# Halved first loads and transposes, tile 1's scores in two sets, and a new order for the opening of a fused attention and MLP kernel

## The chip, the cores and the metric

The kernel runs on one core of a Trainium2 chip. The metric is device time in microseconds (us) of one execution. Before the change three runs took 198.22, 198.23 and 198.53 us, median 198.23.

## The reference

The computation has two parts in a row: an attention in which each query sees 96 local keys and 8 global ones, with a bias that falls with distance, and an MLP with a squared ReLU. Its sizes are 4 batches, 8 heads, 768 positions, head size 64; the MLP has 3072 tokens, 512 columns and 2048 hidden columns.

```python
scores = scale * np.matmul(q, k.transpose(0, 1, 3, 2))
is_global = pos[None, :] < int(n_global)
is_local = (rel >= 0) & (rel < int(n_local))
keep = is_global | is_local
dist = np.where(is_global & ~is_local, float(n_local), np.abs(rel))
bias = -slopes[:, None, None] * dist[None, :, :]
scores = np.where(keep, scores + bias, -1000000000.0)
a = softmax(scores)
x = np.matmul(a, v)            # heads side by side: 3072 x 512
h = x @ w_in
g = np.maximum(h, 0.0) ** 2
return g @ w_out
```

## The kernel before

The 3072 positions are 24 tiles of 128 rows (six per batch). Tile j has its own keys and those of tile j-1, and the eight global keys of its batch; the first tile of a batch (0, 6, 12, 18) has its own keys alone. Two tiles make a block of 256 tokens for the MLP, so there are 12 blocks.

For a tile, the steps are: load q, k and v (fp32 in memory, bf16 on the chip); transpose q and k so that the head size is on the partitions (`tr` on TensorE, here PE, line 530, and the copies `T` out of PSUM, line 546 through the helper of line 416); scores (`sc`, line 619); exp on ScalarE, ACT (`exp`, line 685); for tiles from 3 on a product with a table E of biases on VectorE, DVE (`mul`, line 710); a matmul with v (`pv`, line 769); the division by the sum (`norm`, lines 799 and 800); the transpose of the result x for the MLP (`trx`, line 837, and the copy `xT`). The first three tiles have no product with E: their bias is added on PE (`bias`, line 599) by matmuls of scaled identities `sid` (lines 377 to 382) with a table of distances, in the same PSUM banks as the scores. Each tile takes over eight global keys and values by small copies (`gk`, `gv`).

The MLP of blocks 0 and 1 is computed step by step: a step (`s1`) takes 256 hidden columns of a block, 8 matmuls of 256 columns each or 16 of 128 (line 1083), then `relu` and `sq` evacuate it (lines 886 and 1120); a step needs its piece of w_in, which is loaded in 8 pieces of 256 KB (two of them in two halves). The later blocks use sums of weight parts (`isum`, `wsum`) and seven products in place of eight (`h`, `u`, `c`, `q`, then `s2`).

Tile 0 and 1 differ from the rest: their q and k come over the SP queue as fp32 (lines 319 to 321), 512 KB each, into memory that later holds weight sums (wsum), are cast to bf16 by `cast` (two halves of columns for each of q and k), and are transposed two tiles at a time: 16 transposes for q and 16 for k, then four copies. All other loads are issued by GpSimd (POOL), which casts on the way, and also computes some of the `gv` copies in the same queue.

The order of everything is written out in the table ORDER (lines 57 to 160). Each word is an operation, with the engine behind @ (A for ACT, V for DVE, P for POOL) and the PSUM banks behind the colon; `T.1.3` is the copy of k (1; q is 0) of tile 3. A word adds its instructions to the end of its engine's queue, and each engine works through its queue in order. A word's place against words of other engines has no effect of its own: an instruction waits for its data, for its bank and for what stands ahead in its own queue.

Of the kernel before, what the change touches and what calls it, by code (L numbers as in the profile page):

```python
# [62 lines left out]
ld.win.4.0 ld.win.7.0 pv.2.0:7 pv.2.1:2 gv.2@P ld.win.5.0 ld.win.0.0 ld.win.2.0 tr.1.4:6 norm.2.0 norm.2.1 exp.3.0.0
T.1.4@V s1.0.1:4 s1.0.1#2 sc.4.0:0257 trx.2:3 s1.0.3:1 mul.3.0 relu.0.1@A T.1.5@A pv.3.0:6 mul.3.1 xT.2@V pv.3.1:4
s1.0.3#2 norm.3.0 gk.4@V norm.3.1 exp.4.0.1 exp.4.1.0 exp.4.0.0 exp.4.1.1 mul.4.0 mul.4.1 relu.0.3@A s1.0.4:2
sc.5.0:6547 trx.3:1 s1.0.7:3 xT.3@V sq.0.1@V relu.0.4@A gv.3@A exp.5.1.0 sq.0.3@A exp.5.1.1 s1.1.3:0 relu.0.7@V sq.0.4@A
exp.5.0.0 exp.5.0.1 relu.1.3@V gate.9 sq.0.7@V sq.1.3@A ld.v.4 ld.win.2.1 ld.win.6.0 ld.v.5 ld.win.0.1 s1.1.5:5 s1.1.4:7
# [5 lines left out]
isum.1.0 u.2.0.1@V xs.2.0 s1.1.0:7 tr.1.7:6 s2.0.0.0:2 sc.6.0:45 E0.1 relu.1.2@A u.2.1.1@A exp.6.0.0 exp.6.1.0
relu.1.0@V xs.2.1 sq.1.0@V sq.1.2@A T.1.7@A sq.1.1@V s1.0.6:1 h.2.0.p6 tr.0.7:4 h.2.1.p2:5 relu.0.6@A sq.0.6@A
s2.0.0.1:7 s2.0.1.1 h.2.1.p6 h.2.0.p2:6 s2.0.1.0 s2.0.2.0 mul.6.0 c.2.1.c11 isum.3.1 sum.1.0 c.2.0.c11 sum.1.1 u.2.1.2@A
s2.0.3.0 T.0.7@A sc.7.0:1645 h.2.1.p7 s2.0.2.1 s2.0.4.0 exp.7.0.0 u.2.0.2@A exp.7.0.1 exp.7.1.1 h.2.1.p5:1 s2.0.5.0
pv.6.0:4 s2.0.6.0 s2.0.7.0 isum.2.1 wsum.0.0 wsum.1.0 u.2.1.3@V c.2.1.c22 h.2.1.p3 wsum.0.1 wsum.1.1 xs.2.2 norm.6.0
s2.0.3.1 s2.0.4.1 s2.0.5.1 h.2.0.p7 s2.1.p1.0:5 s2.1.p1.1 s2.0.6.1 s2.0.7.1 s2.1.p2.0:4 o.0.0@A q.2.0.c11@A q.2.1.c11@A
u.2.0.3@A s2.1.p2.1 h.2.0.p4 part.1.p1@A exp.7.1.0 s2.1.p6.0 pv.6.1:2 s2.1.p6.1 part.1.p6@A s2.2.p1.0:6 h.2.1.p4
c.2.0.c21@A s2.2.p1.1 q.2.1.c22@A c.2.1.c12 sum.1.3 wsum.2.0 wsum.2.1 o.0.1@V q.2.0.c21@A c.2.1.c21@A q.2.1.c21@A  # L80
h.2.0.p5:7 o.1.p2 sum.1.2 mul.7.0 gate.11 st.0.0 load.9 T.9 load.8 T.8 load.11 s2.1.p7.0 norm.6.1 gate.12 gate.10
gate.14 mul.7.1 wsum.3.1 isum.2.0 pv.7.1:3 trx.6:1 wsum.3.0 s2.1.p7.1 xT.6@A s2.1.p5.0 gk.7@V c.2.0.c22 part.1.p7@A
pv.7.0:0 q.2.1.c12@A load.10 s2.1.p5.1 norm.7.0 gate.13 q.2.0.c22@A h.2.0.p3 gate.15 s2.1.p4.0 c.2.0.c12 s2.1.p4.1
o.1.p5 q.2.0.c12@A sc.8.0:7012 norm.7.1 o.1.p4@A s2.1.p3.0 sum.2.0 load.12 part.2.p1@A s2.1.p3.1 exp.8.1.0 trx.7:3
sum.2.1 exp.8.0.0 h.3.0.p1:5 exp.8.1.1 xT.7@V h.3.1.p1:0 o.1.p3 exp.8.0.1 h.3.0.p2:7 gk.8@V xs.3.0 u.3.1.1@A sc.9.0:2314
mul.8.0 u.3.0.1@A s2.2.p6.0 xs.3.1 exp.9.0.1 mul.8.1 T.10 h.3.0.p6 exp.9.1.1 h.3.1.p2:1 gv.7@V c.3.0.c11 exp.9.0.0
h.3.1.p6 st.0.1 c.3.1.c11 pv.8.0:4 st.1.1 u.3.1.2@A s2.2.p6.1 norm.8.0 pv.8.1:7 q.3.1.c11@A s2.2.p2.0:2 sum.2.2 gv.8@P
u.3.0.2@A h.3.1.p7 norm.8.1 exp.9.1.0 h.3.0.p5:1 part.2.p6@A xs.3.2 h.3.0.p7 xT.8 u.3.1.3@A mul.9.1 s2.2.p2.1
q.3.0.c11@A mul.9.0 h.3.1.p5:4 u.3.0.3@A st.1.0 s2.2.p7.0 c.3.1.c22 T.12 s2.2.p7.1 c.3.0.c22 pv.9.0:7 q.3.1.c22@A
h.3.1.p3 o.2.p2 q.3.0.c22@A h.3.0.p4 T.11 c.3.1.c12 h.3.0.p3 c.3.0.c21@A norm.9.0 s2.3.p1.0:3 part.2.p7@A s2.3.p1.1  # L90
c.3.0.c12 q.3.1.c12@A pv.9.1:4 h.3.1.p4 q.3.0.c12@A norm.9.1 h.4.0.p1:5 load.15 c.3.1.c21@A gk.9@V sum.3.0 s2.2.p5.0
xT.9 part.3.p1@A q.3.0.c21@A sc.10.0:7140 sum.3.1 s2.2.p5.1 exp.10.1.0 sum.2.3 s2.2.p4.0 exp.10.0.0 gk.10@V o.2.p5
s2.2.p4.1 exp.10.0.1 mul.10.0 load.13 h.4.0.p2:1 u.4.0.1@A s2.3.p6.0 exp.10.1.1 c.4.0.c11 h.4.1.p1:7 gv.9@A s2.2.p3.0
mul.10.1 o.2.p4@A s2.2.p3.1 q.3.1.c21@A sum.3.2 s2.3.p2.0:4 u.4.1.1@A load.14 pv.10.0:0 xs.4.0 pv.10.1:1 gate.17 o.2.p3
s2.3.p6.1 xs.4.1 norm.10.0 s2.3.p2.1 part.3.p6@A h.4.0.p6 q.4.0.c11@A norm.10.1 h.4.1.p6 gv.10@A sum.3.3 xT.10 s2.3.p7.0
u.4.0.2@A xs.4.2 sc.11.0:6201 o.3.p2 u.4.1.2@A h.4.0.p7 exp.11.1.0 st.2.0 h.4.1.p7 T.13 exp.11.0.0 u.4.0.3@V s2.3.p7.1
exp.11.1.1 gate.16 mul.11.0 sc.12.0:26 exp.11.0.1 h.4.0.p4 h.4.1.p2:1 mul.11.1 c.4.0.c21@A s2.3.p5.0 c.4.1.c11
exp.12.1.0 pv.11.0:0 pv.11.1:5 part.3.p7@A norm.11.0 s2.3.p5.1 q.4.1.c11@A h.4.0.p5:1 u.4.1.3@A norm.11.1 h.4.1.p5:6
q.4.0.c21@A gate.20 c.4.0.c22 xT.11 s2.3.p4.0 exp.12.0.0 s2.3.p4.1 gate.18 c.4.1.c22 load.16 h.4.0.p3 o.3.p5 T.15
q.4.1.c22@A h.4.1.p4 mul.12.0 q.4.0.c22@A h.4.1.p3 c.4.0.c12 s2.4.p2.0:0 o.3.p4@A c.4.1.c21@A c.4.1.c12 h.5.0.p1:5  # L100
st.3.1 st.2.1 s2.3.p3.0 u.5.0.1@A q.4.1.c12@V T.14 s2.3.p3.1 q.4.0.c12@A h.5.0.p2:2 o.3.p3 q.4.1.c21@A sc.13.0:1376
c.5.0.c11 h.5.1.p1:4 exp.13.0.0 xs.5.0 s2.4.p2.1 sum.4.0 exp.13.1.0 pv.12.1:2 s2.4.p1.0:1 q.5.0.c11@A xs.5.1 mul.13.0
pv.12.0:3 s2.4.p1.1 u.5.1.1@A gk.13@V sum.4.1 h.5.0.p6 exp.13.0.1 h.5.1.p6 exp.13.1.1 norm.12.0 h.5.0.p5:7 u.5.1.2@A
norm.12.1 h.5.1.p2:6 part.4.p1@A h.5.1.p5:3 xs.5.2 u.5.0.2@A xT.12 mul.13.1 h.5.1.p7 c.5.1.c11 h.5.0.p7 pv.13.0:2 st.3.0
sum.4.2 u.5.0.3@A s2.4.p6.0 T.16 gate.19 s2.4.p6.1 o.4.p2 u.5.1.3@A c.5.0.c22 h.5.0.p4 q.5.1.c11@A pv.13.1:6 norm.13.0
part.4.p6@A s2.4.p5.0 c.5.0.c21@A gv.13@P sum.4.3 h.5.0.p3 q.5.0.c22@A load.17 h.5.1.p4 norm.13.1 q.5.0.c21@A s2.4.p7.0
c.5.0.c12 xT.13 s2.4.p7.1 kl.15@V s2.4.p5.1 c.5.1.c22 part.4.p7@A sc.14.0:2567 q.5.0.c12@A o.4.p5 s2.4.p4.0 kl.14@V
exp.14.0.1 load.18 h.5.1.p3 q.5.1.c22@V c.5.1.c21@A s2.4.p4.1 exp.14.1.1 c.5.1.c12 h.6.0.p1:6 exp.14.1.0 mul.14.1
s2.4.p3.0 exp.14.0.0 s2.4.p3.1 o.4.p4@A mul.14.0 sc.15.0:4735 q.5.1.c12@A xs.6.0 u.6.0.1@A h.6.0.p2:2 xs.6.1 s2.5.p1.0:1
exp.15.0.0 o.4.p3 s2.5.p1.1 exp.15.1.0 c.6.0.c11 st.4.0 h.6.0.p6 exp.15.1.1 T.17 sum.5.0 h.6.0.p5:4 u.6.0.2@A pv.14.0:0  # L110
sum.5.1 pv.14.1:7 exp.15.0.1 h.6.1.p1:2 norm.14.0 part.5.p1@A gv.14@P h.6.0.p7 u.6.1.1@A xs.6.2 load.19 s2.5.p6.0
gate.21 sum.5.2 u.6.0.3@A h.6.1.p6 norm.14.1 q.6.0.c11@A s2.5.p6.1 mul.15.0 q.5.1.c21@A xT.14 h.6.0.p4 part.5.p6@A
# [1345 lines left out]
```

## Time and profile before

| | |
|---|---|
| median of three runs | 198.23 us |
| the profiled execution | 198.52 us |
| its span, first to last instruction | 196.8 us |
| PE busy | 189.8 us (96%) |
| DVE busy | 176.5 us (90%) |
| ACT busy | 163.1 us (83%) |
| POOL busy | 75.2 us (38%) |
| q0, the queue that POOL feeds | 74016 packets, 13.11 MB |
| granted TensorE clock | 0.998 |

All times below are from the start of the span. PE is TensorE's matmul row and PEld its weight load, which overlaps it. A timeline line has the start, the length, the engine, the source line, the operation, the tiles (out<-in), the size and the count; in brackets stands how long the engine had been idle before it and what ended that. When a line holds several instructions its length runs from the first start to the last end. A line of the DMA issues has the number of transfers, their size at the destination (the fp32 source of a cast load is twice as large), and the us from issue to landing.

### The profile page before, as it was taken

The numbers are of one execution on the slowest core, as the hardware profiler recorded it, in microseconds if no ns is written. First come the engines' busy times: TensorE is split into PE (matmuls) and PEld (weight loads), VectorE is DVE, ScalarE is ACT, GpSimd is POOL, SyncE is SP. The second block draws the span as 40 slices with busy tenths as digits, with TensorE's granted clock in tenths as the row PEclk, the third lists the DMA queues.
The fourth block names the chain that finished last, engine by engine and source line by source line (L and its number), as shares of the span: only waits on it lengthen the run. The fifth ranks groups of instructions, "written<-read, shape, count | busy, mean of one in ns | idle before, by whom it ended". The sixth has DMA issues, their size and how long they took to land.

```text
span 196.8 us, 6859 instructions
## 1 busy us (share of the span) xinstructions
PE 189.8 (96%) x2816; PEld 167.8 (85%) x2816; DVE 176.5 (90%) x427; ACT 163.1 (83%) x340; POOL 75.2 (38%) x94
## 2 busy tenths in 40 slices
...
DMA  5999999999699999999999999794996611114023
GB/s 161 194 177 188 183 172 171 205 195 182 112 118 155 189 194 126 190 140 186 140 130 169 110 148 172 166 172 71 115 76 132 160 37 53 30 27 158 5 103 113
DMA packets 105615, 27.18 MB, mean 138 GB/s; under 512 B 95088, under 2 KB 102768, under 8 KB 105584
## 3 DMA queue, kind: packets, MB, share of 16 engines
q0 software_dynamic: 74016, 13.11, 87.2%
...
## 4 chain that ended last, share of the span: by engine, by line
PE 81%; DMA 9%; DVE 5%; ACT 2%; issue 1%; POOL 0%; SPq 0%; DVEq 0%
PE bank L1234 31%; PE bank L972 29%; PE bank L1083 6%; PE bank L619 5%; PE bank L769 4%; PE bank L1365 4%; DMA win<-in_moe_w_in_dram 3%; DMA xT<-x 3%; DMA wsum<-in_k_dram 3%; DVE hsum L1189 1%; ACT at L685 1%; DVE xs L944 1%; ACT qkT L418 1%; DVE hr L1017 1%; DVE x L800 1%
## 5 line engine op out<-in xcount | busy, mean ns | idle before, releaser
L1037 ACT ACTIVATE hs<-hr 128x512 bf16<-128x512 f32 x72 | 44.7, 639 | 5.1 <-DVE hr L1017 4.7
L685 ACT ACTIVATE esc<-bank 128x512 bf16<-128x512 f32 x78 | 43.3, 619 | 1.8 <-PE bank L619 1.4
L1234 PE MATMUL bank<-wsum,hsum 128*128 128x256 bf16 x264 | 36.4, 273 | 0.0
L1234 PEld LDWEIGHTS <-hsum 128*128 128x128 bf16 x360 | 31.9, 98 | 3.5
L1017 DVE CUSTOM_DVE_ANT_0 hr<-bank,early 128x512 f32<-128x512 f32 x45 | 30.4, 685 | 2.2 <-PE bank L972 1.5
L972 PEld LDWEIGHTS <-qk_first 128*128 128x128 bf16 x480 | 29.7, 98 | 1.9 <-DVE xs L944 0.5
L972 PEld LDWEIGHTS <-win 128*128 128x128 bf16 x480 | 29.8, 98 | 1.0
L418 ACT COPY early<-bank 128x512 f32<-128x512 f32 x40 | 23.5, 592 | 4.4 <-PE bank L972 4.3
L710 DVE TENSOR_TENSOR at<-esc,E 128x1024 bf16<-128x1024 bf16 x39 | 26.6, 695 | 0.4 <-ACT esc L685 0.3
L1234 PEld LDWEIGHTS <-hs 128*128 128x128 bf16 x264 | 24.1, 98 | 2.6
L310 POOL DMA_DIRECT2D v<-in_v_dram x18 | 16.1, 892 | 25.0 <-DVE v L468 10.2
L1234 PE MATMUL bank<-wout,hs 128*128 128x256 bf16 x176 | 24.7, 273 | 0.0
L420 POOL COPY v<-v 8x520 bf16<-8x520 bf16 x7 | 5.3, 762 | 49.1 <-PE bank L769 45.4
L972 PE MATMUL bank<-xT,win 128*128 128x128 bf16 x320 | 23.6, 219 | 0.0
L972 PE MATMUL bank<-xs,qk_first 128*128 128x128 bf16 x320 | 22.8, 219 | 0.2 <-DVE xs L944 0.2
L310 POOL DMA_DIRECT2D qk<-in_q_dram x18 | 16.1, 897 | 15.5 <-DMA qkT<-qk 15.1
L800 DVE TENSOR_TENSOR x<-bank,rs 128x256 bf16<-128x256 f32 x48 | 20.4, 424 | 1.8 <-DVE rs L799 0.2
L886 ACT ACTIVATE hr<-bank 128x512 f32<-128x512 f32 x30 | 17.8, 594 | 0.7 <-PE bank L972 0.4
L418 ACT COPY part<-bank 128x256 f32<-128x256 f32 x29 | 10.8, 374 | 8.4 <-PE bank L1234 8.4
L769 PE MATMUL bank<-v,at 128*128 128x65 bf16 x352 | 17.4, 193 | 0.1
L310 POOL DMA_DIRECT2D qk<-in_k_dram x18 | 16.3, 906 | 0.4 <-DMA wout<-in_moe_w_out_dram 0.3
L1083 PE MATMUL bank<-xT,win 128*128 128x256 bf16 (+1 forms) x160 | 16.2, 251 | 0.2
...
## 6 DMA issues: line engine op xcount, KB each, us to landing
out_dram<-o SPq DMA_DIRECT2D x22, 256.0 KB, 3.7
v<-in_v_dram POOLq DMA_DIRECT2D x24, 128.0 KB, 5.2
qk<-in_q_dram POOLq DMA_DIRECT2D x18, 128.0 KB, 5.2
qk<-in_k_dram POOLq DMA_DIRECT2D x18, 128.0 KB, 5.3
wout<-in_moe_w_out_dram POOLq DMA_DIRECT2D x8, 256.0 KB, 8.4
win<-in_moe_w_in_dram POOLq DMA_DIRECT2D x6, 256.0 KB, 6.9
wsum<-in_q_dram SPq DMA_DIRECT2D x1, 512.0 KB, 4.2
wsum<-in_k_dram SPq DMA_DIRECT2D x1, 512.0 KB, 5.5
```

What stands on the lines that cost most here:

```text
L310: nc.gpsimd.dma_start(out=dst, in_=src)
L418: nc.scalar.copy(dst, src)
L685: nc.scalar.activation(out=tiles[tag, j, g][:, odd], in_=tiles.pop(("sc", j, odd, g)).rearrange("p a c -> p (a c)"), func=Act.Exp, scale=s ...
L710: nc.vector.tensor_mul(at, tiles.pop(("esc", j, g)), bias)
L769: nc.tensor.matmul(out=po[:, hi, :], lhsT=tiles["at", j, g][:, odd, at * P : (at + 1) * P], rhs=v_sb[kj][:, h, :], start=(i == 0), stop=(i ...
L800: nc.vector.tensor_tensor(out=x[:, 4 * hf : 4 * hf + 4, :], in0=po[:, :, :D], in1=rs.to_broadcast([P, 4, D]), op=Alu.mult,)
L886: nc.scalar.activation(dst, src, Act.Relu)
L972: nc.tensor.matmul(out=tiles["h", blk, g, bank][:, n], lhsT=left_[:, s, k], rhs=right_[:, k], start=opens and n == 0 and k == 0, stop=k == ...
L1017: nc.vector._custom_dve(TENSOR_ADD_SAT, out=hr, in0=src, in1=tiles.pop(("u", blk, g, i)), s0=float("inf"), s1=0.0,)
L1037: nc.scalar.activation(hs, hr, Act.Square)
L1083: nc.tensor.matmul(out=hT[:, c, cols], lhsT=w_in_sb[s][:, kt, c * P : (c + 1) * P], rhs=tiles["xT", blk][:, kt, cols], start=(kt == 0), st ...
L1234: nc.tensor.matmul(out=tiles["acc", blk, bank][:, cols], lhsT=left_[:, s], rhs=right_[:, cols], start=first and s == 0, stop=s == NSTEP - ...
```

## The change

Five things change, all in the opening of the kernel.

- The q and k of tiles 0 and 1 are loaded in four transfers of four heads each instead of two of eight: q, k, q, k. The order of casts is unchanged in kind, but each cast now waits only for its own half.
- Their transposes are split the same way: 8 for four heads in place of 16, into a bank of their own, and each copy `T` of a half has 256 columns instead of 512. The names get a fourth part, the half: `T.1.0.1` is the copy of k of tile 0, second half.
- Tile 1's scores, one set before, become two: `sc.1.0` for heads 0 to 3 and `sc.1.1` for heads 4 to 7, each waiting only for its own half.
- Four of the eight scaled identities are made by ACT instead of DVE.
- ORDER is written anew up to its 300th word of about 1220; from there on it is the same word for word, except for two loads.

```diff
 ORDER = """
-ld.k.2 ld.v.0 ld.q.2 ld.v.1 ld.q.4 ld.v.2 ld.k.4 ld.win.1.0 cast.0.1@V cast.0.0@V cast.1.0@V bias.0.0:46 bias.1.0:0152
...
+cast.0.0@V cast.1.0@V bias.1.0:47 tr.0.0.0:3 tr.1.0.0:5 bias.1.1:01 T.0.0.0@A T.0.1.0@A cast.0.1@A bias.0.0:23 ones.6
...
-    SETS = {}
+    SETS = {1: [(0,), (1,)]}
...
-    for n, src in ((0, q), (1, k)):
-        nc.sync.dma_start(out=plain[n].rearrange("p (h c) -> p h c", h=H), in_=rows_of_two(src, 0))
-        land["qk"[n], 0] = 4.5 + 1.1 * n
+    for i in range(2):
+        for n, src in ((0, q), (1, k)):
+            h = slice(i * H // 2, (i + 1) * H // 2)
+            nc.sync.dma_start(out=plain[n].rearrange("p (h c) -> p h c", h=H)[:, h], in_=rows_of_two(src, 0)[:, h])
+            land["qk"[n], i] = 4.5 + 1.1 * i + 0.5 * n
...
-    for h in range(H):
+    for h in range(H // 2):
+        nc.scalar.mul(sid[h], ident32, float(slopes[h] / scale))
+    for h in range(H // 2, H):
...
-                for i in range(2) if j == 0 else ():
+                for hs in (range(2), range(2, 4)) if j == 0 else (range(4),):
+                    at = (hs.start // 2,) if j == 0 else ()
...
-                    for pair in range(NPAIR):
+                        for pair in hs:
...
-                            e, qkT[j + i][:, n].rearrange("p a (c r) -> p a c r", r=2),
-                            tiles["tr", n, j][:, :, i * D : (i + 1) * D],
+                                e, qkT[j + i][:, n, h].rearrange("p a (c r) -> p a c r", r=2),
+                                tiles["tr", n, j, *at][:, h, i * D : (i + 1) * D],
...
-        deps = list(parts)
+        every = list(parts)
...
+            deps = [d for d in every if d is None or len(d["name"]) < 4 or d["name"][3] in gs or first]
```

The first place is the start of ACT's queue, from its first activation on (E is the bias table, `at` the exps of tiles 0 to 2, qkT the transposed q and k, wsum the memory that holds q and k as fp32). Before:

```order
L358 ACTIVATE junk<-early 128x1
L386 ACTIVATE E<-pb 128x256 x8
L418 CAST qk_first<-wsum_96 128x512
L418 COPY qkT_81<-bank_110 128x512
L685 ACTIVATE at<-bank_111 128x512
L685 ACTIVATE at<-bank_113 128x512
L685 ACTIVATE at<-bank_109 128x512
```

And now:

```order
L360 ACTIVATE junk<-early 128x1
L380 ACTIVATE early<-ident_100 128x128 x4
L390 ACTIVATE E<-pb 128x256 x8
L422 COPY qkT_81<-bank_110 128x256
L422 COPY qkT_82<-bank_110 128x256
L422 CAST qk_first<-wsum_95 128x512
L698 ACTIVATE at<-bank_114 128x512
L422 COPY qkT_81<-bank_112 128x256
L698 ACTIVATE at<-bank_111 128x512
```

Four identities come ahead of E, two half copies of tiles 0 and 1 and a cast of q's second half follow it, and the first exp is one of tile 1, with one more half copy between it and the next.

The second place is POOL's queue of loads, from the first load to the second copy of global values (v_71 is tile 0's v, v_72 tile 1's, and so on; qk_first with 128x8x128 is a pair of tiles of q or k; win is w_in). Before:

```order
L307 DMA qk_first<-in_k_dram 128x8x128
L307 DMA v_71<-in_v_dram 128x8x64
L307 DMA qk_first<-in_q_dram 128x8x128
L307 DMA v_72<-in_v_dram 128x8x64
L307 DMA qk_first<-in_q_dram 128x8x128
L307 DMA v_73<-in_v_dram 128x8x64
L307 DMA qk_first<-in_k_dram 128x8x128
L307 DMA win<-in_moe_w_in_dram 128x4x256 x2
L307 DMA v_74<-in_v_dram 128x8x64
L420 COPY v_72<-v_71 8x8x65
L307 DMA win<-in_moe_w_in_dram 128x4x256 x2
L420 COPY v_73<-v_71 8x8x65
```

And now:

```order
L307 DMA qk_first<-in_q_dram 128x8x128
L307 DMA qk_first<-in_k_dram 128x8x128
L307 DMA v_71<-in_v_dram 128x8x64
L307 DMA v_72<-in_v_dram 128x8x64
L307 DMA qk_first<-in_k_dram 128x8x128
L307 DMA qk_first<-in_q_dram 128x8x128
L307 DMA v_73<-in_v_dram 128x8x64
L307 DMA v_74<-in_v_dram 128x8x64
L307 DMA win<-in_moe_w_in_dram 128x4x256 x2
L307 DMA win<-in_moe_w_in_dram 128x4x128
L424 COPY v_72<-v_71 8x8x65
L307 DMA win<-in_moe_w_in_dram 128x4x128 x3
```

The v of tile 3 (v_74) has moved ahead of the first piece of w_in, q and k of tiles 2 and 3 come in a row, and two and a half pieces of w_in instead of two stand ahead of the first copy of global values. The pieces themselves are others: 1, 3, 4 and 7 came first before, now 7, 3, 0 and 2.

On PE the steps of the MLP's first layer follow these pieces. Up to tile 4's scores (`sc.4.0`) the table has the same PE work in both kernels, but for one step, `s1.0.1` in its two halves, which stood ahead of `sc.4.0` and now stands much later; the first step is now `s1.0.7`, after `sc.4.0` and `pv.3.0`. On DVE the copies of tile 2's and tile 3's x (`xT.2`, `xT.3`) now stand behind `sq.0.7`, `mul.4.1` and `mul.4.0`.

More of the change, by code (lines that the diff above doesn't have):

```diff
@@ L63 @@
[L63 to L67, printed above, removed]
@@ L73 @@
[L73 to L77, printed above, removed]
@@ L78 @@
[L78 to L112, printed above, removed]
@@ new lines @@
+h.2.1.p5:1 s2.0.1.1 s2.0.2.1 s2.0.5.0 pv.6.0:4 s2.0.6.0 s2.0.7.0 wsum.0.0 isum.2.1 wsum.1.0 h.2.0.p6 u.2.0.2@A u.2.1.3@V
+sum.1.0 c.2.1.c22 isum.3.0 h.2.1.p3 wsum.0.1 sum.1.1 wsum.1.1 xs.2.2 norm.6.0 s2.0.3.1 s2.0.4.1 s2.0.5.1 h.2.0.p7
+s2.1.p1.0:5 s2.1.p1.1 s2.0.6.1 s2.0.7.1 s2.1.p2.0:4 o.0.0@A q.2.0.c11@A q.2.1.c11@A u.2.0.3@A s2.1.p2.1 h.2.0.p4
+part.1.p1@A exp.7.1.0 s2.1.p6.0 pv.6.1:2 s2.1.p6.1 part.1.p6@A s2.2.p1.0:6 h.2.1.p4 c.2.0.c21@A s2.2.p1.1 q.2.1.c22@A
+c.2.1.c12 sum.1.3 wsum.2.0 wsum.2.1 o.0.1@V q.2.0.c21@A c.2.1.c21@A q.2.1.c21@A h.2.0.p5:7 o.1.p2 sum.1.2 mul.7.0
@@ new lines @@
+gate.11 st.0.0 load.9 load.8 T.9 T.8 load.11 s2.1.p7.0 norm.6.1 gate.12 gate.10 gate.14 mul.7.1 wsum.3.1 isum.2.0
+pv.7.1:3 trx.6:1 wsum.3.0 s2.1.p7.1 xT.6@A s2.1.p5.0 gk.7@V c.2.0.c22 part.1.p7@A pv.7.0:0 q.2.1.c12@A load.10 s2.1.p5.1
+norm.7.0 gate.13 q.2.0.c22@A h.2.0.p3 gate.15 s2.1.p4.0 c.2.0.c12 s2.1.p4.1 o.1.p5 q.2.0.c12@A sc.8.0:7012 norm.7.1
+o.1.p4@A s2.1.p3.0 sum.2.0 load.12 part.2.p1@A s2.1.p3.1 exp.8.1.0 trx.7:3 sum.2.1 exp.8.0.0 h.3.0.p1:5 exp.8.1.1 xT.7@V
+h.3.1.p1:0 o.1.p3 exp.8.0.1 h.3.0.p2:7 gk.8@V xs.3.0 u.3.1.1@A sc.9.0:2314 mul.8.0 u.3.0.1@A s2.2.p6.0 xs.3.1 exp.9.0.1
```

220 lines of the change are left out of this document (131 added, 89 removed).

## The prediction

> **What bounds the kernel now.** I read the page first, then busy time by stretch, then the timeline of the first 23 us engine by engine, and last the landings of single loads. Lines of the page (the slices of the DMA engines, and two rows of the issues):
>
> ```profile
> DMA  5999999999699999999999999794996611114023
> ...
> wsum<-in_q_dram SPq DMA_DIRECT2D x1, 512.0 KB, 4.2
> wsum<-in_k_dram SPq DMA_DIRECT2D x1, 512.0 KB, 5.5
> ```
>
> The DMA engines are busy from the second slice on: every load stands in a line. Busy time in three stretches:
>
> ```profile
> core 0: us, PE busy (x) PEld busy (x) DVE busy (x) ACT busy (x) POOL busy (x), PEclk, DMA share, GB/s
> 5.00:17.20 12.20, 10.19 (x223) 8.32 (x221) 8.70 (x29) 10.05 (x23) 8.26 (x11) 1.00 1.84 185
> 17.20:22.40 5.20, 5.11 (x95) 4.28 (x96) 4.80 (x12) 5.20 (x12) 5.20 (x7) 1.00 1.59 191
> 22.40:57.00 34.60, 34.60 (x428) 28.65 (x426) 32.63 (x74) 28.61 (x61) 21.17 (x27) 1.00 1.63 166
> ```
>
> From 22.4 to 57.0 us PE is busy 34.60 of 34.60 us, and 57 us is about where the new order becomes the old one. So the changed stretch can only end earlier if PE is further in its work when this full stretch begins. Before it, PE is busy 10.19 of 12.20 us up to 17.2, and 5.11 of 5.20 after that. The weight loads on PE show what opens the second stretch:
>
> ```profile
> 17.17 0.90 PEld L1083 LDWEIGHTS <-win 128*128 128x128 bf16 x16 [0.26 <-DMA win<-in_moe_w_in_dram]
> 18.17 0.45 PEld L619 LDWEIGHTS <-qkT 64*128 64x128 bf16 x16
> 18.72 0.23 PEld L837 LDWEIGHTS <-x 128*128 128x128 bf16 x4
> 18.91 0.49 PEld L1083 LDWEIGHTS <-win 128*128 128x128 bf16 x8
> 19.47 0.57 PEld L769 LDWEIGHTS <-at 128*128 128x128 bf16 x16
> 19.97 0.47 PEld L1083 LDWEIGHTS <-win 128*128 128x128 bf16 x8
> 20.69 0.77 PEld L1083 LDWEIGHTS <-win 128*128 128x128 bf16 x8 [0.26 <-DMA win<-in_moe_w_in_dram]
> 21.67 0.45 PEld L619 LDWEIGHTS <-qkT 64*128 64x128 bf16 x16 [0.21 <-issue]
> 22.23 0.23 PEld L837 LDWEIGHTS <-x 128*128 128x128 bf16 x4
> 22.41 4.19 PEld L1083 LDWEIGHTS <-win 128*128 128x128 bf16 x39
> ```
>
> Twice PE waits for a piece of w_in. The steps of the first MLP layer (L1083) are the bulk of what PE can do here, and none can start before its piece has landed. ACT is the other candidate:
>
> ```profile
> 3.31 2.56 ACT L386 ACTIVATE E<-pb 128x256 bf16<-128x256 bf16 x8 [1.08 <-DVE pb L375]
> 6.78 0.62 ACT L418 CAST qk_first<-wsum 128x512 bf16<-128x512 f32 x1 [0.91 <-DMA wsum<-in_k_dram]
> 8.11 0.58 ACT L418 COPY qkT<-bank 128x512 bf16<-128x512 bf16 x1 [0.71 <-PE bank L530]
> 9.18 2.70 ACT L685 ACTIVATE at<-bank 128x512 bf16<-128x512 f32 x5 [0.49 <-PE bank L619]
> 11.75 1.10 ACT L418 COPY qkT<-bank 128x512 bf16<-128x512 bf16 x2
> 12.69 2.62 ACT L685 ACTIVATE at<-bank 128x512 bf16<-128x512 f32 x5
> ```
>
> ACT idles 0.91, 0.71 and 0.49 us between its tables E and the first exp at 9.18, and never again up to 15 us. This is what loading in halves can fill. So there are two walls: ACT's chain of exps and copies, and the landing of w_in.
>
> **The change, part by part.** First ACT's chain. Four identities (sid) now stand on ACT ahead of E. The nearest row is another ACT table of 128 columns:
>
> ```profile
> 32.72 0.91 ACT L426 ACTIVATE E<-pb 128x128 bf16<-128x128 bf16 x4
> ```
>
> Four of these take 0.91 us, so four sids end inside the 1.08 us that ACT idles before E (the [1.08 <-DVE pb]): price zero, and if the cover were gone 0.9 us. [...] On DVE four fewer sids let the first cast start when its data are there.
>
> The halved q and k: the two loads of 512 KB, issued at about 0.74 and 1.26 us, land after 4.2 and 5.5 us, at 4.9 and 6.76. Four halves on the same queue should land evenly between: about 4.0, 4.9, 5.8 and 6.7 (an estimate: 1.8 us apart for 512 KB, so 0.9 for 256 KB). Bounds for the first k half: 4.4 (half way, no extra) and 6.76 (all four come together); I take 4.9. PE's prices:
>
> ```profile
> 4.58 1.66 PE L599 MATMUL bank<-pb,early 128*128 128x128 bf16 x16
> 6.17 0.64 PE L530 MATMUL bank<-ident,qk_first 128*64 128x128 bf16 x16
> 7.43 0.64 PE L530 MATMUL bank<-ident,qk_first 128*64 128x128 bf16 x16 [0.61 <-DVE qk_first L422]
> ```
>
> With k's first half at 4.9, its cast (about 0.4) and transposes (half of 16, about 0.4 with the tail) are done at 5.8, when ACT's E ends too. A half copy on ACT has no row; E is 256 columns as well and 8 take 2.56, so about 0.31 each, against 0.48 for a 512-column one in a run (five exps in 2.62 us, whose last alone lasts about 0.7). Bounds 0.24 (half) and 0.48 (no saving); I take 0.31. Two of them and the cast: ACT is free at 6.9. Tile 0's bias matmuls wait for the bank that these copies read (6.5), then take about 0.4, tile 1's first score set 0.4: first exp at about 7.4 instead of 9.18. One half copy and one exp follow; then tile 0's scores wait for the last half copies (the second k half at 6.7, cast, transposes, copies on DVE at about 8.3, scores): the next exp at 9.0. From there ACT has twelve exps and four copies of about 0.48 us, 7.7, two small key copies of about 0.15, and 0.2 us of waiting: tile 3's exps and tile 4's two missing inputs (the k copy and gk.3) are done at about 17.2, so tile 4's scores start at 17.3. In the old kernel they start at 18.17, so ACT's chain is 0.9 us ahead.
>
> But on PE this is no lead. By the table, PE has done the same work before tile 4's scores in both kernels, except that the old one has also done a whole MLP step (s1.0.1, the 16 weight loads from 17.17: 0.90, 1.0 with the switch). 17.3 + 0.9 is 18.2: PE is exactly as far as before.
>
> Now the loads. POOL's queue and landings of single loads, in the order k.4, w_in 1, w_in 3, v.3, w_in 4, w_in 7 (the first landing row below is v.2's, the last w_in 7's):
>
> ```profile
> 6.23 0.88 POOL L307 DMA_DIRECT2D v<-in_v_dram  x1
> 7.10 0.89 POOL L307 DMA_DIRECT2D qk_first<-in_k_dram  x1
> 7.96 1.52 POOL L307 DMA_DIRECT2D win<-in_moe_w_in_dram  x2
> 9.44 0.93 POOL L307 DMA_DIRECT2D v<-in_v_dram  x1
> 14.04 0.62 POOL L420 COPY v<-v 8x520 bf16<-8x520 bf16 x1 [3.67 <-DVE rs L799]
> 14.61 1.50 POOL L307 DMA_DIRECT2D win<-in_moe_w_in_dram  x2
> ```
>
> ```profile
> v<-in_v_dram POOLq DMA_DIRECT2D x1, 128.0 KB, 7.0
> qk_first<-in_k_dram POOLq DMA_DIRECT2D x1, 256.0 KB, 8.9
> win<-in_moe_w_in_dram POOLq DMA_DIRECT2D x1, 256.0 KB, 9.2
> win<-in_moe_w_in_dram POOLq DMA_DIRECT2D x1, 256.0 KB, 9.8
> v<-in_v_dram POOLq DMA_DIRECT2D x1, 128.0 KB, 9.9
> win<-in_moe_w_in_dram POOLq DMA_DIRECT2D x1, 256.0 KB, 6.8
> ```
>
> Issue plus landing: v.2 at 13.2, k.4 at 16.0, w_in 1 at 17.16, w_in 3 at 18.5, v.3 at 19.34, w_in 7 (issued at 15.35) at 22.15. So a w_in piece costs 1.34 us of the line and a v tile 0.84; POOL's wait of 3.67 us for gv.1 didn't empty it. The new line has the same four q and k pieces ahead of w_in, but four v tiles instead of three. Its first w_in piece (7) then lands 0.84 later, at 18.0, w_in 3 at 19.3, w_in 0 at 20.0 and 20.7 (halves), w_in 2 at 21.4 and 22.1. After four w_in pieces both lines have carried the same bytes, and the fourth lands at 22.1 in both.
>
> The sum from 17.3, with the prices of the rows above: scores 0.55 (18.17 to 18.72), pv.3.0 0.25, 18.1; s1.0.7 (landed 18.0) 0.86, 18.95; pv.3.1 0.25, 19.2; s1.0.3 from 19.3, 0.9, 20.2; transposes of tile 2, 0.2; s1.0.0 0.9 with tile 3's transposes 0.2, 21.5; tile 5's scores 0.55, 22.05. The fourth step starts at its landing, 22.1. In the old kernel PE has done the same set (three steps, tiles 0 to 3, tile 5's scores) when its fourth step starts at 22.41. That is 0.3 us; I take 0.2 off it, since the fifth and sixth steps need tile 3's x, which on DVE now stands behind sq.0.7 and two products of tile 4 (0.1), and the split scores of tile 1 and the halved transposes add switches on PE (0.1, bounds 0 and 0.3). Net gain 0.1 us.
>
> Behind 22.4 the work is the same but dealt out otherwise: ACT gives four evacuations away and takes three, DVE the other way round. ACT has slack there (28.61 of 34.60), DVE little (32.63), PE none. I price it at 0, with bounds of -0.2 (small switches saved) and +0.5 (PE waits for DVE). The profiled execution took 198.52 us (span 196.8 and 1.7 around it), at the upper end of the three runs with median 198.23; 198.52 - 0.1 is 198.4 in its own terms, **198.1** against the median.
>
> **The rivals.** *The wall is softer, faster.* k.4 landed 2.8 us after v.2, where a q or k piece should cost about 1.45 (its bytes at the 180 GB/s or so of the first stretch): about 1.2 us of the line went elsewhere once. If that doesn't fall ahead of the new first w_in piece, the pieces land at 16.8, 18.1 and so on, and ACT's chain alone binds: from 17.3 without waits the fourth step comes at 21.9, a gain of 0.5, and 0.9 if my ACT chain is 0.4 too slow: 197.3 to 197.7. For it: nothing ties that loss to k.4 itself. Against it: it falls at a time at which the new line carries q.4 and v.2, both ahead of w_in.
>
> *The halves don't land in order, slower.* If the four pieces share the DMA engines and land together at 6.76, the cover of E is gone and ACT's chain starts late: the first k half has until about 5.2 before it counts (ACT busy with E until 5.87, the DVE copies of tile 1 needed at 6.9), and each us after that is one on tile 4's scores, since nothing on ACT idles later. Late by 0.8 to 1.5 us gives, with 0.3 already eaten at 22.1, 198.6 to 199.3. Against it: the two old loads landed 1.8 us apart though issued 0.5 apart.
>
> *DVE ends last, slower.* The row 22.40:57.00 leaves DVE 2 us; the new order puts a product between the two x copies of tiles 2 and 3 and adds halved copies early. It decides once tile 3's x is more than 0.4 us late; then 198.6 to 198.8.
>
> *The change does what it says and it is hidden*: that is the forecast. The first exp nearly 2 us earlier buys nothing, as w_in lands when it did.
>
> **How the numbers follow.** A measurement of this kernel can tell about 0.2% (0.4 us) from no change. Forecast, 197.8 to 198.6, counted as no change: 0.50. Softer wall: 0.27. Halves together: 0.15. DVE last: 0.08. So faster 0.27, same 0.50, slower 0.23. The range takes in the forecast with its bounds, the upper part of the softer wall and the lower part of the two slower cases: 197.5 to 198.9, leaving out about 0.08 below and 0.12 above. The likeliest case's own range is 197.8 to 198.6.
>
> **What would show it.** Right: the first exp (L698 in the changed kernel) at 7.2 to 7.8; tile 4's scores near 17.3; a wait for w_in before the first L1096 matmul at about 18.0; the fourth step's matmuls within 0.3 of 22.1; PE full from there to 57. Wrong: the first L1096 matmuls well before 17.5 (softer wall); the first cast later than 5.5 (halves together); PE waits on DVE between 22 and 40 us; or a difference that arises behind 57 us, where the order is the old one.

## The result, and the profile after

The changed kernel takes **201.89 us** (median of five runs, 200.38 to 202.10); the kernel before takes 198.23 beside it. The ratio is 1.0163 (95% interval 1.0140 to 1.0185): 3.2 us slower (3.7 by the medians), outside my range. Five runs of before spread over 0.4 us, those of after over 1.7. The profiled run is the fastest of them: 200.38 us, span 198.6.

The page of after, its slices of the DMA engines and its two rows of issues:

```profile
DMA  5999999999999999999999999997995611114023
wsum<-in_q_dram SPq DMA_DIRECT2D x2, 256.0 KB, 4.4
wsum<-in_k_dram SPq DMA_DIRECT2D x2, 256.0 KB, 5.2
```

The medians of 4.4 and 5.2 us hide the point, for a first and a second half are not alike. The rows of single transfers, in the order of issue (q, k, q, k), and SP's own queue (start, length):

```profile
wsum<-in_q_dram SPq DMA_DIRECT2D x1, 256.0 KB, 3.0
wsum<-in_k_dram SPq DMA_DIRECT2D x1, 256.0 KB, 3.3
wsum<-in_q_dram SPq DMA_DIRECT2D x1, 256.0 KB, 5.8
wsum<-in_k_dram SPq DMA_DIRECT2D x1, 256.0 KB, 7.1
```

```profile
0.74 0.46 SPq L322 DMA_DIRECT2D wsum<-in_q_dram  x1
1.26 0.49 SPq L322 DMA_DIRECT2D wsum<-in_k_dram  x1
1.80 0.50 SPq L322 DMA_DIRECT2D wsum<-in_q_dram  x1
2.34 0.51 SPq L322 DMA_DIRECT2D wsum<-in_k_dram  x1
```

Issue plus landing: the first halves are there at 3.7 and 4.6 us, earlier than I said, the second ones at 7.6 and 9.4, where before had all of q at 4.9 and all of k at 6.75. ACT and DVE show who waits:

```profile
7.58 0.62 ACT L422 CAST qk_first<-wsum 128x512 bf16<-128x512 f32 x1 [0.71 <-DMA wsum<-in_q_dram]
8.10 0.59 ACT L698 ACTIVATE at<-bank 128x512 bf16<-128x512 f32 x1
10.23 0.37 ACT L422 COPY qkT<-bank 128x256 bf16<-128x256 bf16 x1 [1.54 <-DVE qkT L426]
10.50 2.26 ACT L698 ACTIVATE at<-bank 128x512 bf16<-128x512 f32 x4
```

```profile
9.44 0.43 DVE L426 CAST qk_first<-wsum 128x512 bf16<-128x512 f32 x1 [2.24 <-DMA wsum<-in_k_dram]
```

The first exp comes at 8.10 (before 9.18), but the next work of ACT waits 1.54 us for a chain that begins with the cast of k's second half. The third exp, the first of tile 0, is the second in the row at 10.50: it starts at about 11.2, where I had forecast 9.0. PE from there on:

```profile
8.25 0.41 PE L537 MATMUL bank<-ident,qk_first 128*64 128x128 bf16 x8 [0.45 <-ACT qk_first L422]
9.92 0.86 PE L537 MATMUL bank<-ident,qk_first 128*64 128x128 bf16 x24 [1.26 <-DVE qk_first L426]
...
19.28 0.23 PE L631 MATMUL bank<-qkT 64*128 64x128 bf16 x2 [1.04 <-ACT qkT L422]
...
20.14 1.04 PE L1096 MATMUL bank<-xT,win 128*128 128x256 bf16 x8
...
24.14 1.07 PE L1096 MATMUL bank<-xT,win 128*128 128x128 bf16 x16
```

Tile 4's scores start at 19.28 (forecast 17.3, before 18.17), still waiting for ACT, and the first MLP step stands behind them without a wait for w_in. The fourth step (24.14) starts 1.7 us later than in before (22.41), nearly the whole 1.8 us by which the span is longer. The three stretches in which before was read:

```profile
5.00:17.20 12.20, 9.84 (x198) 7.47 (x198) 6.49 (x23) 9.52 (x23) 7.60 (x11) 1.00 1.85 182
17.20:22.40 5.20, 4.16 (x93) 3.74 (x88) 4.50 (x14) 5.03 (x13) 4.92 (x8) 1.00 1.78 181
22.40:57.00 34.60, 34.60 (x437) 28.66 (x435) 32.62 (x70) 26.83 (x58) 20.34 (x26) 1.00 1.53 166
```

PE is busy 0.35 us less in the first and 0.95 less in the second; from 22.4 to 57.0 it is full again, 34.60 of 34.60. The loss lies ahead of 22.4. What this one profile doesn't tell is why the other four runs are 0.9 to 1.7 us longer still.

### The profile page after: what moved, and what is told of

It reads as the page before. It is cut to its first block, busy times and chain, and to the rows that moved or that the text cites. A ratio compares the mean times of both kernels' runs of the same rounds, so it can differ in the third digit from the quotient of the medians.

```text
span 198.6 us, 6856 instructions
## 1 busy us (share of the span) xinstructions
PE 190.4 (96%) x2816; PEld 168.2 (85%) x2816; DVE 175.9 (89%) x425; ACT 163.0 (82%) x345; POOL 75.3 (38%) x95
## 4 chain that ended last, share of the span: by engine, by line
PE 83%; ACT 6%; DVE 4%; DMA 4%; issue 1%; SPq 1%; DVEq 0%; ACTq 0%
PE bank L1247 31%; PE bank L985 31%; PE bank L1096 7%; PE bank L631 6%; PE bank L782 4%; DMA wsum<-in_k_dram 4%; PE bank L1378 3%; ACT at L698 2%; ACT esc L698 1%; ACT qkT L422 1%; DVE hr L1030 1%; DVE wsum L1167 1%; SPq L322 1%; ACT early L422 1%; ACT hs L1050 1%
## 5 line engine op out<-in xcount | busy, mean ns | idle before, releaser
L422 ACT COPY early<-bank 128x512 f32<-128x512 f32 x39 | 22.9, 593 | 3.4 <-PE bank L985 3.3
L899 ACT ACTIVATE hr<-bank 128x512 f32<-128x512 f32 x33 | 19.2, 595 | 1.4 <-ACT hs L1050 0.5
L782 PE MATMUL bank<-v,at 128*128 128x65 bf16 x352 | 17.3, 193 | 0.4 <-ACT at L698 0.4
L782 PEld LDWEIGHTS <-at 128*128 128x128 bf16 x352 | 15.1, 98 | 1.5 <-issue 0.5
```

Of the source, the lines that this page charges most:

```text
L422: nc.scalar.copy(dst, src)
L782: nc.tensor.matmul(out=po[:, hi, :], lhsT=tiles["at", j, g][:, odd, at * P : (at + 1) * P], rhs=v_sb[kj][:, h, :], start=(i == 0), stop=(i ...
L899: nc.scalar.activation(dst, src, Act.Relu)
```

## The experiments

Three theories stood at first. A: the second halves land late because POOL's loads get in among them, and that delays the opening. B: the new order costs the time, whatever lands when. C: SP's queue itself pauses between its second and third load. All ratios below are against the kernel before, timed beside each.

| kernel | median us | ratio (95%) | tile 4's scores | span of that run |
|---|---|---|---|---|
| after | 201.89 | 1.0163 (1.0140 to 1.0185) | 19.28 | 198.6 |
| whole loads in after | 201.37 | 1.0133 (1.0105 to 1.0161) | 20.22 | 200.1 |
| POOL 2 us late in after | 199.85 | 1.0083 (1.0063 to 1.0103) | 18.06 | 197.9 |
| after, two queues | 199.04 | 1.0033 (1.0016 to 1.0050) | 17.87 | 197.1 |
| half loads in before | 202.58 | 1.0210 (1.0190 to 1.0231) | | 200.2 |
| idle matmuls in after | 200.73 | 1.0117 (1.0097 to 1.0136) | 20.33 | 199.6 |
| one half on ACT in after | 199.65 | 1.0075 (1.0047 to 1.0102) | 18.57 | 197.8 |
| identities on ACT in before | 198.43 | 1.0000 (0.9989 to 1.0012) | | 196.4 |
| two queues, a copy to DVE | 199.77 | 1.0073 (1.0056 to 1.0090) | 18.09 | 198.1 |
| two queues, identities on DVE | 198.53 | 1.0007 (0.9997 to 1.0018) | 17.34 | 196.9 |
| two queues, both | 198.93 | 1.0033 (1.0020 to 1.0046) | 17.56 | 197.1 |
| half loads and idle matmuls in before | 201.92 | 1.0175 (1.0145 to 1.0204) | | 201.9 |

**Whole loads in the changed kernel.**

```diff
-    for i in range(2):
-        for n, src in ((0, q), (1, k)):
...
+    for n, src in ((0, q), (1, k)):
+        nc.sync.dma_start(out=plain[n].rearrange("p (h c) -> p h c", h=H), in_=rows_of_two(src, 0))
+        for i in range(2):
...
```

> The changed kernel with its four half loads of q and k put back to two whole loads; the new order, the halved casts, transposes and copies and the two score sets stay. Theory A (the second halves of q and k land late, 7.55 and 9.41 us, because they share the DMA engines with POOL's first loads, and that delays the whole opening): q lands near 4.9 and k near 6.75 as in the kernel before, ACT's 1.54 us of idling ahead of its second exp goes, tile 4's scores start near 18.1 instead of 19.28, and the time is 198.0 to 199.7. Theory B (the new order itself, with its four v tiles ahead of w_in and its switches on PE, costs the time): the landings change but the time stays at 200.9 to 202.

The number is B's, but the run does not speak for B. In the new order PE must transpose k's first half before the last twelve bias matmuls and tile 1's scores, and with a whole k (at 6.98 us) it does so only at 7.48: tile 4's scores come at 20.22, later than in after. (Part of that is a stretch at half clock, which the profile of after doesn't have.) The order needs its halves, so this kernel separates nothing. It did show something else, in the stretches of 3.41 us in which the records of the granted clock change:

```profile
4.33:7.74 3.41, 1.40 (x22) 0.80 (x19) 1.02 (x6) 2.71 (x9) 3.41 (x4) 1.00 1.54 236
7.74:11.15 3.41, 3.41 (x44) 2.66 (x40) 1.35 (x4) 0.60 (x1) 3.01 (x5) 0.50 2.12 168
11.15:14.57 3.42, 3.21 (x70) 2.44 (x66) 2.12 (x5) 3.22 (x8) 0.28 (x1) 1.00 2.03 171
```

PE was busy 1.40 of 3.41 us, and in the next 3.41 us the granted clock (the third column from the right) is 0.50.

**POOL late.** Six idle iotas ahead of POOL's first load.

```diff
+    idle = const([P, 2, P], I32, "idle")
+    for i in range(6):
+        nc.gpsimd.iota(idle, pattern=[[-P, 2], [-1, P]], base=0, channel_multiplier=1)
```

> The changed kernel with six idle iotas (about 2 us) on POOL ahead of its first load; the four half loads stay. Theory A (sharing with POOL's loads): POOL's packets start when SP's are nearly through, the second halves land near 5.8 and 6.8 us instead of 7.55 and 9.41, the exps run on without the 1.54 us gap, and the time is 198.3 to 200.0, though POOL's line starts later. Theory C (the SP queue itself pauses between its second and third load, whoever else loads): the pause near 4.0 to 4.75 us stays, the second halves land near 6.5 and 7.5 at best, and the time is 199.5 to 201. Theory B (order): 201 to 203.

With POOL out of the way (first issue at 3.48 instead of 1.34) the second halves land at 6.2 and 6.9 (issued as before, at 1.80 and 2.34):

```profile
wsum<-in_q_dram SPq DMA_DIRECT2D x1, 256.0 KB, 4.4
wsum<-in_k_dram SPq DMA_DIRECT2D x1, 256.0 KB, 4.6
```

That is only 0.4 and 0.2 us behind the 5.8 and 6.7 of the prediction: with POOL's packets out of the way, four halves on one queue land nearly as I had them, and the other 1.4 and 2.5 us of after's lateness go with POOL's loads. The median is 199.85, inside A's bounds and C's alike, and 2 us below after although POOL's whole line starts 2 us late. C has a small part: the DMA engines' stretch from 4 to 5 us is thin here too. The same stretch (4.00:5.00), one kernel per fence, first before, then after, then POOL late:

```profile
4.00:5.00 1.00, 1.00 (x7) 0.56 (x6) 1.00 (x6) 1.00 (x5) 1.00 (x3) 1.00 1.17 322
```

```profile
4.00:5.00 1.00, 1.00 (x4) 0.45 (x3) 1.00 (x4) 1.00 (x5) 1.00 (x2) 1.00 0.69 126
```

```profile
4.00:5.00 1.00, 1.00 (x4) 0.45 (x3) 1.00 (x3) 1.00 (x4) 1.00 (x2) 1.00 0.71 187
```

The last column is GB/s: 322 before, 126 after, 187 with POOL late. So SP's queue does falter once the first two of its four loads are through, and in after POOL's packets get in just there. From 4.0 to 5.5 us the queues carried, before (first fence) and after (second):

```profile
q1 hardware_dynamic: 923, 0.47, 118.2%
```

```profile
q1 hardware_dynamic: 328, 0.17, 49.7%
q0 software_dynamic: 211, 0.05, 37.1%
```

Before, not one packet of POOL's queue ran in that time. The other traces agree: in the four kernels with four loads on SP's queue and POOL's first issue at 1.34, POOL's first packet ran at about 4.0 us, and in no other kernel before 5.0.

**Two queues.** The halves of k are issued by ACT, so no queue has more than two loads. The kernel was run once for the first of the two expectations below (198.90 us) and seven times for the second.

```diff
-            nc.sync.dma_start(out=plain[n].rearrange("p (h c) -> p h c", h=H)[:, h], in_=rows_of_two(src, 0)[:, h])
+            (nc.sync, nc.scalar)[n].dma_start(out=plain[n].rearrange("p (h c) -> p h c", h=H)[:, h], in_=rows_of_two(src, 0)[:, h])
```

> The changed kernel with the halves of k issued by ACT instead of SP, so that no queue issues more than two. ACT's table load, identities and E then start about 1 us later, so this is a look at the landings, not a proposal. If the late issue of the third and fourth load (1.80 and 2.34 us) is what lets POOL's packets in (theory A), all four halves land by 7.0 us. If the engines pause whatever the issue times (theory C), the last half lands after 8 us. The time by theory A: 199.5 to 201.5 (1 us of ACT lost, the late landings gone); by C: 201 to 203.

> The kernel of the two queues (k's halves issued by ACT) again, now timed. Theory A (the late second halves were the loss): 198.6 to 199.2 in nearly every run, with a clock of 0.997 or more, that is within 0.6 us of the kernel before although ACT starts 1 us late. Theory B (the new order costs on its own, the one run of 198.9 was lucky): 199.5 to 201.

```profile
4.00:5.00 1.00, 1.00 (x4) 0.46 (x3) 0.60 (x3) 1.00 (x5) 1.00 (x3) 1.00 1.17 327
```

327 GB/s, no faltering. q's halves land at 4.6 and 6.3, k's last half at 6.95 (issued near 1.25, 5.7 us), and seven runs lie within 198.89 and 199.36. Of after's 3.2 us, 0.65 is left: A holds, B (199.5 to 201) falls for all but that rest. The single run lies below what A had allowed for it (199.5 to 201.5): ACT's later start costs less than the 1 us that I had put down. One thing isn't separated: the edit also issues the last half 1.1 us earlier (1.25 instead of 2.34), though it lands 2.5 us earlier.

**Half loads in the kernel before**, nothing else changed.

```diff
-    for n, src in ((0, q), (1, k)):
-        nc.sync.dma_start(out=plain[n].rearrange("p (h c) -> p h c", h=H), in_=rows_of_two(src, 0))
-        land["qk"[n], 0] = 4.5 + 1.1 * n
+    for i in range(2):
+        for n, src in ((0, q), (1, k)):
+            h = slice(i * H // 2, (i + 1) * H // 2)
+            nc.sync.dma_start(out=plain[n].rearrange("p (h c) -> p h c", h=H)[:, h], in_=rows_of_two(src, 0)[:, h])
+            land["qk"[n], 0] = 4.5 + 1.1 * n
```

> The kernel before with its two loads of q and k split into the four half loads and nothing else changed. Theory A: the second halves land at 7 to 9.5 us instead of 4.9 and 6.75, all copies of tiles 0 and 1 and the first exp come 1.5 to 2.7 us later, and the time is 199.5 to 201. Theory B (order): 198.0 to 198.7, no change.

The split of the loads alone costs 4.2 us, more than A's 1.2 to 2.7: B gave no change and is out. Part of the surplus over A is the clock:

```profile
5.91:9.32 3.41, 1.45 (x31) 1.13 (x29) 1.38 (x3) 0.00 (x0) 2.45 (x3) 1.00 1.65 193
9.32:12.74 3.42, 2.27 (x40) 1.61 (x34) 1.98 (x3) 1.92 (x4) 1.63 (x2) 0.50 2.03 172
12.74:16.15 3.41, 3.41 (x47) 2.53 (x44) 2.24 (x9) 2.53 (x6) 0.00 (x0) 0.50 1.83 181
```

PE waits 1.96 us for q's second half, then 0.47 for k's, is busy 1.45 of 3.41 us, and then runs two stretches at half clock; all four runs have a mean granted clock of 0.983. In after, three of five runs have 0.989 to 0.991 and the profiled one 1.0. Its stretch with the wait:

```profile
6.00:9.41 3.41, 2.21 (x40) 1.58 (x36) 0.76 (x2) 1.76 (x4) 2.60 (x3) 1.00 1.60 199
```

2.21 of 3.41 was enough to keep the clock. This is theory D: a second loss behind the first, which depends on how the stretches of 3.41 us fall on PE's wait. They begin at different times in the profiles: at 4.33 and 7.74 us with whole loads in after, at 5.91 and 9.32 with half loads in before, at 6.00 and 9.41 in after. 1.40 and 1.45 us of work in a stretch did not keep the clock for the next one, and 2.27 us of work at half clock did not bring it back.

**Idle matmuls in PE's wait.** D's test: five in after (the bank is free), then eight in the kernel before with half loads.

```diff
+                        if (n, at) == (0, (1,)):
+                            for _ in range(5):
+                                nc.tensor.matmul(out=banks[6], lhsT=zero[:, :P], rhs=zero, start=True, stop=True)
```

> The changed kernel with five idle matmuls of 512 columns on PE (into a free bank) between the transposes of q's second half and those of k's second half, where PE waits from 8.66 to 9.92 us. Theory D (behind the late landing there is a second loss: PE stands idle for so much of a 3.4 us stretch that its granted clock is halved in the next one, in some runs and not in others): no run has a granted clock below 0.997, the runs lie within 0.6 us of each other, and the median falls from 201.89 to 200.2 to 200.9, near the profiled 200.38, in which the clock was not halved. Rival E (the runs differ because the loads land differently, the clock has no part): the median stays at 201.4 to 202.3. If the idle matmuls hold up PE, it rises above 202.

All six runs keep a clock of 0.997 or more and the median falls by 1.2 us to 200.73, so E, which had it stay, is out. The profile's stretch with the wait:

```profile
8.30:11.72 3.42, 2.19 (x36) 1.36 (x37) 1.05 (x3) 1.56 (x4) 1.06 (x2) 1.00 2.01 174
```

Of these 2.19 us 1.03 are idle matmuls (from 9.89 on): without them 1.16 would be left, less than the 1.45 that lost the clock above. D's bound on the spread (0.6 us) fails: the runs lie 1.15 us apart. Landings that vary from run to run can do that: with the same four loads as in after, the second halves in this profile took

```profile
wsum<-in_q_dram SPq DMA_DIRECT2D x1, 256.0 KB, 6.8
wsum<-in_k_dram SPq DMA_DIRECT2D x1, 256.0 KB, 8.1
```

and landed at 8.6 and 10.5 us, 1 us later than in after's. The idle matmuls didn't cause that, as PE runs them only once q's second half is there.

```diff
+                    if (n, j) == (0, 0):
+                        for _ in range(8):
+                            nc.tensor.matmul(out=banks[3], lhsT=zero[:, :P], rhs=zero, start=True, stop=True)
```

> The kernel before with the four half loads (202.58 us, granted clock 0.983 in all four runs, PE idle from 6.70 to 8.66 us in the profile) and, in addition, eight idle matmuls of 512 columns on PE ahead of its first transposes, about 1.7 us of that wait. Theory D (the halved clock is a loss of its own): the clock stays at 0.996 or above in every run and the time falls to 200.2 to 201.4; what is left over the kernel before is the late landing alone. Rival E (the late landing alone costs 4.3 us, the clock only shows it): the time stays at 202 to 203.

Half a miss. Four of six runs keep the clock (201.19 to 202.08 us), two do not (202.86 and 203.72, both 0.983): the same kernel, 0.8 us or more between the groups. The profiled one is of the second group. Here both second halves came 1 us later than in the kernel without idle matmuls (at 8.5 and 10.4 us), the idle matmuls ran in the stretch before, and the one behind them had 1.27 us of work:

```profile
8.10:11.52 3.42, 1.27 (x32) 0.95 (x32) 2.38 (x5) 0.62 (x1) 0.95 (x2) 1.00 1.92 180
11.52:14.93 3.41, 2.77 (x44) 2.18 (x44) 1.56 (x3) 1.82 (x4) 0.93 (x2) 0.50 2.04 171
```

So D holds, but its price is not separated from the landings: the medians of the two groups (203.29 and 201.54) lie 1.75 us apart, and the profiled run with the halved clock is also one with later halves. With the clock kept, the late landing costs this kernel 3.2 us, a little more than the 1.9 to 3.1 that I had put down for it.

**One half on ACT**: only q's second half.

```diff
+            (nc.scalar if (i, n) == (1, 0) else nc.sync).dma_start(out=plain[n].rearrange("p (h c) -> p h c", h=H)[:, h], in_=rows_of_two(src, 0)[:, h])
```

> The changed kernel with only the second half of q issued by ACT, the other three halves by SP. Theory A: all halves land by 7.0 us, ACT loses only about 0.5 us ahead of its identities, which its later wait hides, tile 4's scores start near 17.6, and the time is 198.0 to 198.8, no change against the kernel before, as w_in's landing then ends the waits. Theory C (a third load on SP's queue pauses it, whatever the first queue had before): the third load on SP lands after 7.5 and the time is 199.5 to 201.

Neither. ACT's load, issued at 0.73 and landed at 5.3 us, is under way at the same time as k's first half,

```profile
wsum<-in_k_dram SPq DMA_DIRECT2D x1, 256.0 KB, 5.0
```

which now lands at 6.2 us (issued at 1.26) instead of 4.6; the first exp comes at 8.81, tile 4's scores at 18.57. The last half lands at 7.1, and from 4 to 5 us the engines move 336 GB/s although SP's queue has three loads, so C's strict form falls as well. It seems to count not only when all have landed, but also that the half that is needed first comes first; no run tests that alone.

**Identities on ACT in the kernel before**, and back on DVE in the two-queue kernel.

```diff
-    for h in range(H):
+    for h in range(H // 2):
+        nc.scalar.mul(sid[h], ident32, float(slopes[h] / scale))
+    for h in range(H // 2, H):
```

> The kernel before with only the four identities moved from DVE to ACT. My price of zero: 198.1 to 198.6, E still starts at 3.3 us. Rival (they push E back): E starts at 4.2, and the time is 198.6 to 199.2.

Price zero, ratio 1.0000 (0.9989 to 1.0012), E still at 3.31:

```profile
2.41 0.91 ACT L378 ACTIVATE early<-ident 128x128 bf16<-128x128 f32 x4 [0.17 <-DVE ident L370]
3.31 2.56 ACT L388 ACTIVATE E<-pb 128x256 bf16<-128x256 bf16 x8
```

> The kernel of the two queues with all eight identities back on DVE, so that ACT's table E ends 0.9 us earlier, near 5.75 instead of 6.6, and DVE's first cast 0.5 to 0.8 us later. Theory F: the first exp comes at 7.5 to 8.1, the next exps hang on k's second half (landing near 6.6) and tile 4's scores come 0 to 0.4 us earlier than 17.87: 198.6 to 199.1. Rival H (DVE's casts are what ACT and PE wait for): tile 4's scores come later than 17.87 and the time is 199.1 to 199.8.

Here ACT begins 1.14 us late, as it issues two loads first, so the cover of the four identities is gone, and taking them off ACT saves 0.5 us: 198.53, ratio 1.0007 (0.9997 to 1.0018). Tile 4's scores come 0.53 us earlier, a little more than F's 0 to 0.4. With the halves on time and E on time, the new order costs nothing that can be measured and gains nothing. ACT in this kernel, from the second exp to tile 4's scores:

```profile
8.66 2.16 ACT L696 ACTIVATE at<-bank 128x512 bf16<-128x512 f32 x4
...
11.28 0.63 ACT L696 ACTIVATE at<-bank 128x512 bf16<-128x512 f32 x1
...
12.24 2.12 ACT L696 ACTIVATE at<-bank 128x512 bf16<-128x512 f32 x4
...
14.62 2.19 ACT L696 ACTIVATE esc<-bank 128x512 bf16<-128x512 f32 x4
```

The third exp, the first of tile 0, is the second in the row at 8.66 and starts at about 9.25. From it on there are twelve, as the prediction has it; the thirteen that the next expectation speaks of are counted from the second one. PE's row behind them, and further down:

```profile
17.34 0.23 PE L629 MATMUL bank<-qkT 64*128 64x128 bf16 x2 [1.04 <-ACT qkT L420]
...
20.66 0.39 PE L848 MATMUL bank<-ident,x 128*128 128x128 bf16 x4
21.15 0.84 PE L1094 MATMUL bank<-xT,win 128*128 128x128 bf16 x12
22.48 1.07 PE L1094 MATMUL bank<-xT,win 128*128 128x128 bf16 x16
```

The fourth step starts at 22.48, before at 22.41.

**A copy to DVE**, alone and with the identities.

```diff
-exp.2.0.1 T.1.5@A exp.3.1.0
+exp.2.0.1 T.1.5@V exp.3.1.0
```

> The kernel of the two queues with one full copy (k of tile 5, T.1.5, 0.47 us of ACT's time) given to DVE. In the two-queue kernel tile 4's scores start at 17.87 with a wait of 1.04 us on ACT, and the time is 199.04, 0.6 over the kernel before. Theory F (what is left of the loss is ACT's chain of exps and copies up to tile 4's scores: I counted twelve exps from the second one on where the order has thirteen): tile 4's scores start at 17.4 and the time falls by 0.3 to 0.5, to 198.5 to 198.8. Rival G (what is left comes from DVE or the landing of w_in behind tile 4's scores): tile 4's scores start earlier, the time stays at 198.9 to 199.2.

> Both edits on the kernel of the two queues: T.1.5 on DVE and all identities on DVE. Theory F: the gains add, tile 4's scores start at 17.0 to 17.4, and the time is 198.2 to 198.7, where the landing of w_in (17.7, 19.0, 19.7, 20.5 us in the two-queue kernel) begins to end the waits. Rival H: 198.8 to 199.5.

A miss on both counts (198.93 lies in H's range, but not because of the casts). The copy takes 0.69 us on DVE, and at its place in the queue it stands ahead of the divisions of tiles 0 and 1; PE then waits for the x of these tiles,

```profile
15.90 0.84 PE L850 MATMUL bank<-ident,x 128*128 128x128 bf16 x8 [0.78 <-DVE x L813]
```

and tile 4's scores come later, not earlier (18.09 alone, with a wait for DVE). That ACT's chain sets tile 4's scores is shown by the identities (0.53 us earlier on ACT, 0.53 on tile 4's scores, 0.5 in the time), not by this pair, and a wrong count of exps, which F gave as its ground, has no part in it. No version that was run beats the kernel before.

## Why the prediction was wrong, point by point

- **The landing of the halves** is the step that failed: "Four halves on the same queue should land evenly between: about 4.0, 4.9, 5.8 and 6.7". The first two came early, the second two at 7.6 and 9.4 us (8.6 and 10.5 in the profile with idle matmuls). I had treated the queue as a line with a fixed rate, and left out what stands beside it: POOL's loads, of which no packet ran before 5.5 us in the kernel before and which now ran beside SP's from 4.0 us on (211 packets to 328 by 5.5), and a queue that falters behind the second of its four loads (126 to 187 GB/s where before has 322). With POOL late the second halves came at 6.2 and 6.9, so the faltering without POOL delays them by only 0.2 to 0.4 us. The rival "The halves don't land in order" was the nearest, but it had the first half of k late, with a first cast after 5.5 us as its sign, and 6.76 as the time by which all four have landed. In after the first cast starts at 4.20; it is the second halves that are late, by 1.8 and 2.7 us, and no case that I had named reaches 201.9.
- **A term was missing: the granted clock.** The row of before is all nines, and I read no risk in it. In the three profiles where PE's wait left 1.45 us or less of a 3.41 us stretch busy, the next one ran at 0.50. By the ratios this is about 0.9 us of the 3.2 (1.0163 with it, 1.0117 with idle matmuls), though landings that vary blur the split.
- **The chain of ACT** was sized right and started late. From the third exp to tile 4's scores I had 8.3 us (9.0 to 17.3); it took 8.1 in after (11.2 to 19.28) and 8.1 with the halves on time (9.25 to 17.34, two queues and identities on DVE). In after the third exp is 2.2 us late, tile 4's scores 2.0, and the fourth step 2.0 (24.14 against 22.1). The first exp, forecast for 7.4, came at 8.10, as ACT's cast of q's second half stands ahead of it and had to wait for its landing.
- **From 17.3 on** the time came out nearly as forecast: with tile 4's scores at 17.34 the kernel takes 0.1 us more than before (interval -0.1 to +0.4), where I had said 0.1 less. The pieces of w_in landed a little before I had them (17.7, 19.0, 19.7 and 20.5 in the two-queue kernel, against 18.0, 19.3, 20.0 and 20.7), so the softer wall is not there. But w_in binds less than I had it: in after PE never waits for it, and with 17.34 it waits once, for about 0.3 us, when the second half of w_in's piece 0 lands (between the rows at 20.66 and 21.15). The fourth step starts at 22.48 (said: 22.1, old 22.41), and not at its landing: PE's own work from tile 4's scores on takes 4.86 us (19.28 to 24.14 in after, with no wait), where I had 4.6 without waits. The 0.2 us that I had taken off the gain covers most of this.
- **The identities on ACT** cost nothing (measured 1.0000), and what they cost without cover was 0.5 us where I had said 0.9. In after each of them lasts 0.29 to 0.31 us, but starts 0.2 us after the one before it, so four took 0.91 us again.
- **DVE last**: not seen. From 22.4 to 57 DVE is busy 32.62 us (before 32.63) and PE full.

What stays open: why SP's queue falters behind the second of four loads, though with three loads on it and one on ACT's it doesn't (336 GB/s); how much of the 3.2 us is the clock's; and why POOL's queue, whose first load was issued at the same 1.34 us, got no packet through before 5.5 us in one kernel and its first at 4.0 us in the other. The runs show that, and not its cause.
